# Second score matmul on 64 rows, two neighbouring tiles on the two halves of the array

## The chip, the cores and the metric

The kernel runs on one core of one Trainium2 chip. The metric is the device time of one execution in microseconds (us), here the median of 3 runs. Engines are named as in the profile: PE (TensorE matmul) and PEld (its weight loads), DVE (VectorE), ACT (ScalarE), POOL (GpSimd), SP (SyncE, which only issues transfers here).

## What is computed

An attention without softmax feeds two dense layers, one after the other, each of which widens 256 to 2048 columns and narrows back. Two batches of 3008 tokens go through it, in float32:

```python
scores = (1.0 / S) * np.matmul(z, z.transpose(0, 2, 1))   # z: (2, 3008, 64)
attn = np.maximum(scores, 0.0) ** 2
x = (u * np.matmul(attn, v)).reshape(B * S, D)            # u, v: (2, 3008, 256)
r = np.maximum(x @ moe_w_in, 0.0)                         # 256 -> 2048
x = (moe_s * (r * r) + moe_b) @ moe_w_out                 # 2048 -> 256
h = x @ moe2_w_in
out = (h * (1.0 / (1.0 + np.exp(-1.702 * h)))) @ moe2_w_out
```

Only the scores are touched by the change. The dot product behind a score has 64 terms, half of the array's 128 rows.

## The kernel before

**Two parts for each operand.** Matmul operands are of a rounded type (F32R). A value is therefore split into a high part (the value cast to F32R) and a low part (value minus high), and a product is summed from products of parts.

**Scores.** z of one batch is cut into 6 chunks of 512 tokens. `split_z` brings z of a chunk into `zt`, whose rows 0 to 63 and 64 to 127 both hold the transposed chunk. From it comes `zk`, the key operand: `high()` casts all 128 rows on ACT, and `low(cols)` (line 407) then subtracts in rows 64 to 127 on DVE, so that rows 0 to 63 hold the high part and rows 64 to 127 the low part of the same tokens. `queries` makes `zq`, the query operand, with two halves along the free axis: `zq[:, 0]` is the high part in both row halves, `zq[:, 1]` the low part in both. A score tile is 128 keys (tile t of 4 in chunk kc) by 512 queries (chunk c), built by two matmuls into one `ps` buffer (lines 566 to 568): with h = 0 the contraction over 128 rows gives (high + low of k) times high of q, with h = 1 it gives (high + low of k) times low of q.

**After the scores** (class `Fresh`, method `up`), each tile runs a chain: Relu with the scale, out of ps, on ACT (line 572); Square on ACT (575); the cast to the high part `hi` on ACT (582; on DVE, line 580, for the first four tiles); the low part `lo` on DVE (587, or 591 on half the rows for the last, short tile of a batch). For kc other than c, DVE also transposes the tile (616, method `turn`); four of them are parked in HBM and come back later as tile (kc, c) mirrored, for which class `Turned` only needs the two parts (666 on ACT, 670 on DVE). Method `down` then adds a tile's share of the output: `add_up` issues 6 matmuls (lines 507, 508, 512) into the accumulators accA or accB of the open session (one session is one query chunk). A tile's `down` is written 5 steps (`LAG`) behind its `up`.

**Order.** No engine's order is written by hand. `write_list` lists operations with costs, reads and writes (`put`, through `scalar`, `vector`, `matmuls`, `moves`), and `ordered` places them: a simulated clock for each engine, the PE line nearly in the order written (any of its next 16 operations that is ready may go), every other engine by what can start first, then by the latest due time. A negative `due` is added to an operation's latest time, a positive one replaces it. Buffers are counted too, among them 4 of kind `ps` and 56 `cell`. Decoding of the layers' weights (lines 716 to 803 on DVE, 719 and 794 on ACT) is `free` work, spread over 45 to 380 us for the first layer and 240 to 400 and 480 to 900 us for the second.

**Stages in the profile.** Attention of batch 0 fills the time up to about 230 us, that of batch 1 up to about 460 us. The first session of a batch has Fresh tiles only, and v of all chunks is split then (484 on ACT, 488 on DVE). Two dense layers follow.

Of the kernel before, what the change touches and what calls it, by code (L numbers as in the profile page):

```python
# [11 lines left out]
ALU = mybir.AluOpType  # L12
# [219 lines left out]
def attention_mlp_mlp_kernel(  # L232
# [13 lines left out]
    nc = tc.nc  # L246
# [3 lines left out]
    P = 128  # L250
# [75 lines left out]
    def vector(n, f, reads=(), writes=(), new=(), fast=False, **more):  # L326
        put("DVE", 0.065 + (0.00056 if fast else 0.00105) * n, 0.14, f, reads, writes, new, **more)
# [16 lines left out]
    def matmuls(count, n, f, reads=(), adds=(), writes=(), new=()):  # L344
        put("PE", count * (n / 2400 + 0.0133), 0.27, f, reads, writes, new, adds)
# [12 lines left out]
    def load_z(bb, t):  # L358
        n, z0, key = width(t), begin(bb, t), ("zr", bb, t)

        def tile_of():
            if key not in T:
                T[key] = cell(f"zr_{bb}_{t}").rearrange("p (t a) -> p t a", a=32)
            return T[key]

        fs = {"SP": [], "ACT": []}
        for i in range(4):
            q = slice(32 * i, 32 * i + 32)
            col = slice(32 * (i % 2), 32 * (i % 2) + 32)
            pieces = [(slice(0, n // 32), z0, n)]  # L370
            if n < CH:
                pieces.append((slice(n // 32, CH // 32), z0 + n - TAIL, TAIL))
            for cols, r0, r in pieces:
                on_act = (bb, t) == (0, 0) and i % 2

                def f(q=q, col=col, cols=cols, r0=r0, r=r, eng=nc.scalar if on_act else nc.sync):
                    eng.dma_start(
                        out=tile_of()[q, cols, :], in_=z[bb, r0 : r0 + r, col].rearrange("(t b) a -> b t a", b=32)
                    )

                fs["ACT" if on_act else "SP"].append(f)
        due = 0.0 if (bb, t) == (0, 0) else -16.0 if bb else None
        moves(64 * len(fs["SP"]), fs["SP"], (), [key], [(key, "cell")], run=128, due=due)
        if fs["ACT"]:
            moves(128, fs["ACT"], (), [(key, 1)], (), engine="ACT", run=128, due=due)

    def split_z(bb, t):
        zr, zt, zk = [(x, bb, t) for x in ("zr", "zt", "zk")]

        def turn():  # L390
            T[zt] = cell(f"zt_{bb}_{t}")
            if t < LASTC:
                nc.vector.transpose(
                    out=T[zt].rearrange("p (t g a) -> p t g a", t=4, g=4),
                    in_=T[zr].rearrange("p (g t) a -> p t g a", g=4),
                )
            else:
                nc.vector.transpose(out=T[zt], in_=T[zr].rearrange("p t a -> p (t a)"))

        def high():  # L400
            T[zk] = cell(f"zk_{bb}_{t}", F32R)
            if early and t:
                nc.vector.tensor_copy(out=T[zk], in_=T[zt])
            else:
                nc.scalar.copy(out=T[zk], in_=T[zt])

        def low(cols):
            nc.vector.tensor_tensor(out=T[zk][64:, cols], in0=T[zt][64:, cols], in1=T[zk][64:, cols], op=ALU.subtract)

        early = bb == 0 and t < EARLY  # L410

        vector(CH, turn, [zr] + ([(zr, 1)] if (bb, t) == (0, 0) else []), [zt], [(zt, "cell")])
        if (bb, t) == (0, 0):

            def go():
                nc.gpsimd.tensor_copy(out=going, in_=T[zt][:, :1])

            put("POOL", 0.1, 0.15, go, [zt], [("go",)])
        if early and t:
            vector(CH, high, [zt], [zk], [(zk, "cell")], fast=True)  # L420
        else:
            scalar(CH, high, [zt], [zk], [(zk, "cell")])
        if (bb, t) == (0, 0):
            vector(P, lambda: low(slice(0, P)), [zt, zk], [zk])
            vector(CH - P, lambda: low(slice(P, CH)), [zt, zk], [(zk, "rest")])
        else:
            vector(CH, lambda: low(slice(0, CH)), [zt, zk], [zk])

    def queries(bb, t):
        zt, zq = [(x, bb, t) for x in ("zt", "zq")]  # L430
# [12 lines left out]
    def load_v(bb, c):  # L443
        key, k0 = ("vr", bb, c), begin(bb, c)

        def tile_of():
            if key not in T:
                T[key] = big_tile(f"vr_{bb}_{c}").rearrange("p (t d) -> p t d", t=TPC)
            return T[key]

        pieces = []
        if c < LASTC:
            for g in range(4):
                pieces.append((slice(32 * g, 32 * g + 32), slice(0, TPC), k0 + g * P, P, "(t j) d -> j t d", dict(j=32)))
        else:
            pieces.append((slice(0, P), slice(0, 3), k0, 3 * P, "(t p) d -> p t d", dict(p=P)))
            for half in range(2):
                pieces.append((slice(64 * half, 64 * half + 64), slice(3, 4), k0 + 3 * P, TAIL, "(t p) d -> p t d", dict(p=TAIL)))
        first = (bb, c) == (0, 0)
        queue = "POOL" if bb == 0 and c else "SP"  # L460
        fs = {"SP": [], "ACT": [], "POOL": []}
        for x, (rows_, ts, r0, r, how, dims) in enumerate(pieces):
            issuer = "ACT" if first and x % 2 else queue

            def f(rows_=rows_, ts=ts, r0=r0, r=r, how=how, dims=dims, issuer=issuer):
                eng = dict(SP=nc.sync, ACT=nc.scalar, POOL=nc.gpsimd)[issuer]
                eng.dma_start(out=tile_of()[rows_, ts, :], in_=v[bb, r0 : r0 + r, :].rearrange(how, **dims))

            fs[issuer].append(f)
        due = 0.05 if first else None  # L470
        gate = [("go",)] if queue == "POOL" else []
        moves(128 * len(fs[queue]), fs[queue], gate, [key], [(key, "big")], engine=queue, run=1024, slow=1.5, due=due)
        if fs["ACT"]:
            moves(256, fs["ACT"], (), [(key, 1)], (), engine="ACT", run=1024, slow=1.5, due=due)
# [77 lines left out]
    class Fresh:  # L552
# [7 lines left out]
        def up(self):  # L560
            bb, n, kc, t, c = self.bb, self.n, self.kc, self.t, self.c
            zk, zq = ("zk", bb, kc), ("zq", bb, c)

            def scores():
                T[self.p] = ps.tile([P, CH], F32, tag=tag("ps"), name="ps_s")
                k = T[zk][:, t * P : (t + 1) * P]
                for h in range(2):
                    nc.tensor.matmul(T[self.p][:, :n], k, T[zq][:, h, :n], start=h == 0, stop=h == 1)  # L568

            def relu():  # L570
                T[self.a] = cell("a")
                nc.scalar.activation(out=T[self.a][:, :n], in_=T[self.p][:, :n], func=AF.Relu, scale=1.0 / S)  # L572

            def square():
                nc.scalar.activation(out=T[self.a][:, :n], in_=T[self.a][:, :n], func=AF.Square)  # L575

            def high():
                T[self.hi] = cell("hi", F32R)
                if first:
                    nc.vector.tensor_copy(out=T[self.hi][:, :n], in_=T[self.a][:, :n])  # L580
                else:
                    nc.scalar.copy(out=T[self.hi][:, :n], in_=T[self.a][:, :n])  # L582

            def low():
                T[self.lo] = cell("lo", F32R)
                a, hi, lo = [T[x][:, :n] for x in (self.a, self.hi, self.lo)]
                nc.vector.tensor_tensor(out=lo, in0=a, in1=hi, op=ALU.subtract)  # L587

            def low_half():
                hi = T[self.hi][64:, :n]  # L590
                nc.vector.tensor_tensor(out=hi, in0=T[self.a][64:, :n], in1=hi, op=ALU.subtract)

            early = (bb, kc, c) == (0, 0, 0)
            rest = [(zk, "rest")] if early and t else []
            matmuls(2, n, scores, [zk, zq] + rest, (), [self.p], [(self.p, "ps")])
            first = early and t < FIRST
            scalar(n, relu, [self.p], [self.a], [(self.a, "cell")])
            scalar(n, square, [self.a], [self.a])
            if first:
                vector(n, high, [self.a], [self.hi], [(self.hi, "cell")], fast=True)  # L600
            else:
                scalar(n, high, [self.a], [self.hi], [(self.hi, "cell")])
            if self.whole:
                vector(n, low, [self.a, self.hi], [self.lo], [(self.lo, "cell")])
            else:
                vector(n, low_half, [self.a, self.hi], [self.hi])
            if kc != c:
                self.turn()

        def turn(self):  # L610
            key, t = ("T", self.bb, self.kc, self.c), self.t
# [1089 lines left out]
```

## Time and profile before

| | us |
|---|---|
| median of 3 runs | 1388.39 (1387.8 to 1388.91) |
| the profiled execution | 1388.55 |
| its span, first to last instruction | 1386.5 |
| PE busy | 1377.9 |
| DVE busy | 1312.0 |
| ACT busy | 1187.4 |

The granted TensorE clock was 1.00 all through the span. Busy time of PE is time in which any matmul's record is open; records overlap, as the next matmul starts before the one ahead has left the array. The time of an execution is the span and some 2 us around it.

### The profile page before, as it was taken

The page shows a single profiled execution, that of the slowest core. Times are in us where ns is not written, and L with a number is a line of the kernel's source. Part 1 is how long each engine was busy: PE and PEld are TensorE (multiplying, and loading weights), DVE is VectorE, ACT ScalarE, POOL GpSimd, SP SyncE. Part 2 cuts the span into 40 slices and gives each one's busy share as a digit, 9 for nine tenths or more (in the row PEclk, how much of TensorE's full clock was granted, in tenths as well). Part 3 has the DMA queues.
Part 4 walks back from the last instruction along what each step waited for, and adds up shares of the span by engine and source line. Part 5 has one row for each costly group of instructions (what it writes and reads, how often), then busy time and mean ns, then how long its engine had stood idle before and what let it go on. Part 6 is the DMA issues. An engine that isn't in the chain of part 4 may idle for free.

```text
span 1386.5 us, 20220 instructions
## 1 busy us (share of the span) xinstructions
PE 1377.9 (99%) x6146; PEld 1149.4 (83%) x6146; DVE 1312.0 (95%) x2329; ACT 1187.4 (86%) x2304; POOL 197.4 (14%) x325
## 2 busy tenths in 40 slices
PE   9999999999999999999999999999999999999998
PEld 6788889888888888888888888988888888888897
DVE  8999999999999789999999999999999999999997
ACT  8999777999868698999989898988788796978785
POOL 4243221253321001001000100000010101010010
PEclk9999999999999999999999999999999999999999
DMA  9798998699998567677767575865767575655553
GB/s 198 241 285 272 304 279 218 184 306 279 294 312 295 177 214 254 209 234 260 271 218 249 189 267 193 288 219 202 237 212 262 171 259 166 235 183 200 178 186 107
DMA packets 187149, 322.62 MB, mean 233 GB/s; under 512 B 85408, under 2 KB 117728, under 8 KB 183200
## 3 DMA queue, kind: packets, MB, share of 16 engines
q1 hardware_dynamic: 160016, 241.68, 54.5%
q0 software_dynamic: 24288, 78.91, 17.4%
q10 hardware_dynamic: 2736, 0.74, 0.3%
q8 instruction: 49, 0.80, 0.2%
q14 instruction: 60, 0.49, 0.1%
HBM read 244.19 MB, written 77.07 MB: 232 GB/s over the span
## 4 chain that ended last, share of the span: by engine, by line
PE 99%; DVE 1%; ACT 0%; issue 0%; DVEq 0%
PE ps_b L1119 9%; PE ps_d L1119 9%; PE ps_c L1119 9%; PE accB L1312 7%; PE ps_b L1312 6%; PE ps_d L1312 6%; PE ps_s L568 5%; PE accA L508 5%; PE accA L507 5%; PE ps_a L1119 5%; PE accB L508 5%; PE accB L507 5%; PE accA L512 5%; PE accB L512 4%; PE ps_c L1312 4%; PE accA L1312 4%
## 5 line engine op out<-in xcount | busy, mean ns | idle before, releaser
L1242 DVE TENSOR_TENSOR lo<-g_c,hi 128x512 fp32r<-128x512 f32 (+1 forms) x540 | 344.9, 672 | 6.1 <-ACT hi L1238 5.3
L1238 ACT CAST hi<-g_c 128x512 fp32r<-128x512 f32 (+1 forms) x540 | 310.4, 616 | 10.6 <-DVE g_c L1227 9.0
L572 ACT ACTIVATE a<-ps_s 128x512 f32<-128x512 f32 (+1 forms) x168 | 102.7, 616 | 37.1 <-PE ps_s L568 36.8
L1119 PE MATMUL ps_b<-op_t,up 128*128 128x512 f32 (+1 forms) x432 | 120.6, 387 | 0.2 <-DVE g_c L1193 0.2
L1119 PE MATMUL ps_d<-op_t,up 128*128 128x512 f32 (+1 forms) x432 | 120.6, 387 | 0.0
L507 PE MATMUL accA<-hi,v 128*128 128x512 f32 x288 | 112.2, 390 | 0.9 <-DVE hi L580 0.9
L587 DVE TENSOR_TENSOR lo<-a,hi 128x512 fp32r<-128x512 f32 (+1 forms) x156 | 104.8, 672 | 8.5 <-ACT hi L582 7.9
L508 PE MATMUL accA<-hi,v 128*128 128x512 f32 x288 | 112.4, 390 | 0.1
L575 ACT ACTIVATE a<-a 128x512 f32<-128x512 f32 (+1 forms) x168 | 110.7, 660 | 0.6
L508 PE MATMUL accB<-hi,v 128*128 128x512 f32 (+1 forms) x288 | 109.8, 381 | 0.0
L507 PE MATMUL accB<-hi,v 128*128 128x512 f32 (+1 forms) x288 | 109.7, 381 | 0.0
L1205 ACT ACTIVATE g_c<-g_c 128x512 f32<-128x512 f32 (+1 forms) x144 | 89.3, 624 | 22.1 <-DVE g_c L1193 21.5
L1227 DVE TENSOR_TENSOR g_c<-g_c,g_c 128x512 f32<-128x512 f32 (+1 forms) x156 | 105.1, 674 | 1.3
L582 ACT CAST hi<-a 128x512 fp32r<-128x512 f32 (+1 forms) x164 | 105.3, 643 | 0.5
L568 PE MATMUL ps_s<-zq,zk 128*128 128x512 f32 (+1 forms) x336 | 102.3, 389 | 0.1
L1312 PE MATMUL accB<-hi,d 128*128 128x512 f32 (+1 forms) x312 | 95.0, 386 | 0.0
L1119 PEld LDWEIGHTS ps_b<-op_t,up 128*128 128x128 f32 x432 | 80.1, 188 | 17.3 <-DVE g_c L1193 1.4
L1119 PEld LDWEIGHTS ps_d<-op_t,up 128*128 128x128 f32 x432 | 79.8, 188 | 17.4 <-ACT s_u L1168 2.1
L1208 ACT ACTIVATE g_c<-g_c 128x512 f32<-128x512 f32 (+1 forms) x144 | 88.7, 630 | 0.5
L635 POOL DMA_DIRECT2D H<-T x120 | 66.1, 557 | 137.9 <-DVE T L616 115.5
L512 PE MATMUL accA<-lo,v 128*128 128x512 f32 x276 | 85.1, 390 | 0.0
L616 DVE STREAM_TRANSPOSE T<-a 128x512 f32<-128x512 f32 x120 | 84.0, 702 | 0.2
(180 smaller groups left out, 3479.2 us busy)
## 6 DMA issues: line engine op xcount, KB each, us to landing
up<-uf SPq DMA_DIRECT2D x96, 896.0 KB
H<-T POOLq DMA_DIRECT2D x120, 256.0 KB, 6.3
R<-H SPq DMA_DIRECT2D x30, 1024.0 KB
d<-dw SPq DMA_DIRECT2D x114, 256.0 KB
d_s<-df1s SPq DMA_DIRECT2D x54, 256.0 KB
d_s<-df0s SPq DMA_DIRECT2D x72, 128.0 KB
f<-rows SPq DMA_DIRECT2D x18, 512.0 KB
d_s<-df0s SPq DMA_DIRECT2D x36, 256.0 KB
```

Source lines behind the costliest of these rows:

```text
L507: nc.tensor.matmul(T[k][:, :n], w[:, 0, cols], T[hi][:, :n], **start_flags(k, fresh))
L508: nc.tensor.matmul(T[k][:, :n], w[:, 1, cols], T[hi][:, :n], **start_flags(k, ()))
L512: nc.tensor.matmul(T[k][:, :n], w[:, 0, cols], T[lo][:, :n], **start_flags(k, ()))
L568: nc.tensor.matmul(T[self.p][:, :n], k, T[zq][:, h, :n], start=h == 0, stop=h == 1)
L575: nc.scalar.activation(out=T[self.a][:, :n], in_=T[self.a][:, :n], func=AF.Square)
L582: nc.scalar.copy(out=T[self.hi][:, :n], in_=T[self.a][:, :n])
L587: nc.vector.tensor_tensor(out=lo, in0=a, in1=hi, op=ALU.subtract)
L1119: nc.tensor.matmul(to[:, :n], a[h], y[:, g, :n], start=first and j == 0, stop=False, skip_group_check=True)
L1227: nc.vector.tensor_tensor(out=self.get(to), in0=self.get(x), in1=self.get(y), op=ALU.subtract)
L1238: nc.scalar.copy(out=T[keys[0]][:, :n], in_=self.get(c))
L1242: nc.vector.tensor_tensor(out=T[keys[1]][:, :n], in0=self.get(c), in1=T[keys[0]][:, :n], op=ALU.subtract)
L1312: nc.tensor.matmul(to[:, :n], w[:, h, cols], g[:, :n], start=first and j == 0, stop=False, skip_group_check=True)
```

## The change

A tile's second score matmul (h = 1) uses 64 rows alone: the high part of k times the low part of q. The product of the two low parts, which rows 64 to 127 had added, is dropped. So that the second matmuls of two neighbouring tiles can name different halves of the array, odd tiles of a chunk have their parts in `zk` the other way round: `low(odd)` subtracts in rows 0 to 63 for odd tiles and in rows 64 to 127 for even ones, as two instructions of 256 columns (three for the first chunk). The even tile's `scores` issues only its full matmul. The odd tile's issues its own full one, then the even tile's second on rows 0 to 63, then its own second on rows 64 to 127. The chain behind both tiles (`later`) is listed after the odd tile's scores, the even tile's first. For the planner the even tile's operation counts one matmul, the odd one's two. Due times of the first z and v transfers become -100 and -50 instead of 0 and 0.05.

```diff
-        due = 0.0 if (bb, t) == (0, 0) else -16.0 if bb else None
+        due = -100.0 if (bb, t) == (0, 0) else -16.0 if bb else None
...
-        def low(cols):
-            nc.vector.tensor_tensor(out=T[zk][64:, cols], in0=T[zt][64:, cols], in1=T[zk][64:, cols], op=ALU.subtract)
+        def low(odd, xs=slice(0, 2)):
+            rows_ = slice(0, 64) if odd else slice(64, 128)
+            to, src = [T[x][rows_].rearrange("p (x y k) -> p y x k", y=2, k=P)[:, odd, xs] for x in (zk, zt)]
+            nc.vector.tensor_tensor(out=to, in0=src, in1=to, op=ALU.subtract)
...
-            vector(P, lambda: low(slice(0, P)), [zt, zk], [zk])
-            vector(CH - P, lambda: low(slice(P, CH)), [zt, zk], [(zk, "rest")])
+            vector(P, lambda: low(0, slice(0, 1)), [zt, zk], [zk])
+            vector(HALF, lambda: low(1), [zt, zk], [(zk, "rest")])
+            vector(P, lambda: low(0, slice(1, 2)), [zt, zk], [(zk, "rest")])
         else:
-            vector(CH, lambda: low(slice(0, CH)), [zt, zk], [zk])
+            for odd in range(2):
+                vector(HALF, lambda odd=odd: low(odd), [zt, zk], [zk])
...
-        due = 0.05 if first else None
+        due = -50.0 if first else None
...
+            def product(x, rows_, h):
+                k = T[zk][rows_, x.t * P : (x.t + 1) * P]
+                nc.tensor.matmul(T[x.p][:, :n], k, T[zq][rows_, h, :n], start=h == 0, stop=h == 1)
+
             def scores():
                 T[self.p] = ps.tile([P, CH], F32, tag=tag("ps"), name="ps_s")
-                k = T[zk][:, t * P : (t + 1) * P]
-                for h in range(2):
-                    nc.tensor.matmul(T[self.p][:, :n], k, T[zq][:, h, :n], start=h == 0, stop=h == 1)
+                product(self, slice(0, P), 0)
+                if t % 2:
+                    product(other, slice(0, 64), 1)
+                    product(self, slice(64, P), 1)
...
+            def later():
+                scalar(n, relu, [self.p], [self.a], [(self.a, "cell")])
+                scalar(n, square, [self.a], [self.a])
...
             early = (bb, kc, c) == (0, 0, 0)
+            first = early and t < FIRST
             rest = [(zk, "rest")] if early and t else []
-            matmuls(2, n, scores, [zk, zq] + rest, (), [self.p], [(self.p, "ps")])
-            first = early and t < FIRST
-            scalar(n, relu, [self.p], [self.a], [(self.a, "cell")])
-            scalar(n, square, [self.a], [self.a])
...
+            other = self.session.steps[self.session.steps.index(self) - 1] if t % 2 else None
+            matmuls(2 if t % 2 else 1, n, scores, [zk, zq] + rest, [other.p] if t % 2 else (), [self.p], [(self.p, "ps")])
+            self.later = later
+            if t % 2:
+                other.later()
+                later()
```

## Rows read from the trace of the kernel before

**Rows 1.** The page: busy us (share) of each engine; the chain that ended last.
```profile
PE 1377.9 (99%) x6146; PEld 1149.4 (83%) x6146; DVE 1312.0 (95%) x2329; ACT 1187.4 (86%) x2304; POOL 197.4 (14%) x325
...
PE 99%; DVE 1%; ACT 0%; issue 0%; DVEq 0%
```

**Rows 2.** Windows: length, then busy us (xinstructions) of PE, PEld, DVE, ACT, POOL.
```profile
50.00:100.00 50.00, 50.00 (x222) 41.41 (x221) 49.84 (x96) 48.39 (x94) 17.62 (x31) 1.00 0.85 259
100.00:250.00 150.00, 150.00 (x680) 127.16 (x679) 142.00 (x273) 118.89 (x234) 37.17 (x61) 1.00 0.90 268
250.00:300.00 50.00, 50.00 (x222) 41.44 (x221) 49.88 (x104) 49.64 (x104) 18.18 (x32) 1.00 0.77 236
300.00:450.00 150.00, 150.00 (x672) 125.71 (x671) 143.43 (x271) 124.46 (x239) 44.91 (x72) 1.00 0.94 293
450.00:500.00 50.00, 50.00 (x232) 42.89 (x231) 38.32 (x72) 34.16 (x65) 1.96 (x3) 1.00 0.53 186
500.00:930.00 430.00, 429.83 (x1924) 359.68 (x1923) 422.59 (x738) 400.95 (x777) 29.48 (x44) 1.00 0.70 238
```

**Rows 3.** Timeline at 54 us: start, length, engine, line, operation.
```profile
54.09 0.62 PE L568 MATMUL ps_s<-zq,zk 128*128 128x512 f32 x2
...
54.54 0.39 PE L507 MATMUL accA<-hi,v 128*128 128x512 f32 x1
54.55 0.19 PEld L508 LDWEIGHTS accA<-hi,v 128*128 128x128 f32 x1
```

**Rows 4.** Instructions of the ps_s tiles: Relu, one for each score tile (ns, starts, forms).
```profile
L572 ACT ACTIVATE a<-ps_s x168: 536/600/737, 7.8 to 444.7; 128x512 f32<-128x512 f32 x160, 128x448 f32<-128x448 f32 x8
```

**Rows 5.** Timeline at 10 us: a matmul that waited, and the next one.
```profile
9.99 0.50 PE L507 MATMUL accA<-hi,v 128*128 128x512 f32 x1 [0.88 <-DVE hi L580]
...
10.33 0.40 PE L508 MATMUL accA<-hi,v 128*128 128x512 f32 x1
```

**Rows 6.** Timeline at 490 us: four matmuls of 64 columns, and the next load.
```profile
490.17 0.53 PE L900 MATMUL ps_c<-ones,wt 128*128 128x64 f32 x4
...
490.50 0.30 PEld L1312 LDWEIGHTS accB<-hi,d 128*128 128x128 f32 x2
```

**Rows 7.** Timeline of ACT, 19 to 50 us: the first and the last of 16 Relus.
```profile
21.64 0.60 ACT L572 ACTIVATE a<-ps_s 128x512 f32<-128x512 f32 x1
...
49.56 0.66 ACT L572 ACTIVATE a<-ps_s 128x512 f32<-128x512 f32 x1
```

**Rows 8.** Windows of line 568 alone: length, busy us (xmatmuls), loads, clock, DMA.
```profile
0.00:50.00 50.00, 15.68 (x52) 9.53 (x52) 1.00 0.90 218
...
250.00:300.00 50.00, 16.62 (x54) 10.13 (x54) 1.00 0.77 236
```

**Rows 9.** DVE groups from 250 to 300 us: busy us, mean ns, idle before.
```profile
L803 DVE TENSOR_TENSOR forms<-wf,forms 128x256 fp32r<-128x256 f32 (+2 forms) x6 | 2.7, 447 | 0.0
L781 DVE TENSOR_TENSOR ws<-wf 128x128 f32<-128x128 f32 x8 | 2.1, 278 | 0.0
```

**Rows 10.** Timeline of the first 10 us: from the first transfers to the first lo.
```profile
0.74 0.91 SPq L377 DMA_DIRECT2D zr<-in_z_dram  x2
...
1.70 0.95 SPq L467 DMA_DIRECT2D vr<-in_v_dram  x2
...
6.51 0.76 DVE L408 TENSOR_TENSOR zk<-zt,zk 64x128 fp32r<-64x128 f32 x2
...
6.91 2.20 PE L568 MATMUL ps_s<-zq,zk 128*128 128x512 f32 x8
...
7.76 1.09 ACT L572 ACTIVATE a<-ps_s 128x512 f32<-128x512 f32 x2 [0.34 <-PE ps_s L568]
...
9.97 0.69 DVE L587 TENSOR_TENSOR lo<-a,hi 128x512 fp32r<-128x512 f32 x1
```

**Rows 11.** Lines 408 and 488 on DVE: count, min/median/max ns, first and last start.
```profile
L408 DVE TENSOR_TENSOR zk<-zt,zk x13: 289/690/692, 6.5 to 261.9; 64x512 fp32r<-64x512 f32 x11, 64x128 fp32r<-64x128 f32 x1, 64x384 fp32r<-64x384 f32 x1
...
L488 DVE TENSOR_TENSOR v<-vr,v x48: 379/417/426, 7.3 to 279.2; 128x256 fp32r<-128x256 f32 x48
```

More of the change, by code (lines that the diff above doesn't have):

```diff
@@ L591, in low_half @@
                 nc.vector.tensor_tensor(out=hi, in0=T[self.a][64:, :n], in1=hi, op=ALU.subtract)
+            def later():
+                scalar(n, relu, [self.p], [self.a], [(self.a, "cell")])
+                scalar(n, square, [self.a], [self.a])
+                if first:
+                    vector(n, high, [self.a], [self.hi], [(self.hi, "cell")], fast=True)
+                else:
+                    scalar(n, high, [self.a], [self.hi], [(self.hi, "cell")])
+                if self.whole:
+                    vector(n, low, [self.a, self.hi], [self.lo], [(self.lo, "cell")])
+                else:
+                    vector(n, low_half, [self.a, self.hi], [self.hi])
+                if kc != c:
+                    self.turn()
             early = (bb, kc, c) == (0, 0, 0)
+            first = early and t < FIRST
             rest = [(zk, "rest")] if early and t else []
-            matmuls(2, n, scores, [zk, zq] + rest, (), [self.p], [(self.p, "ps")])
-            first = early and t < FIRST
-            scalar(n, relu, [self.p], [self.a], [(self.a, "cell")])
-            scalar(n, square, [self.a], [self.a])
[L599 to L608, printed above, removed]
+            other = self.session.steps[self.session.steps.index(self) - 1] if t % 2 else None
[4 more added lines that the diff above has]
+                later()
         def turn(self):
```

## The prediction, made before the changed kernel was run

> **What bounds the kernel now.** I read the page's busy shares and its chain of work first [rows 1]: PE is busy for 1377.9 of 1386.5 us, and the chain that ended last is PE for 99%. The windows by stage [rows 2] then show PE without a hole from 50 to 500 us, so each slot of PE that goes in the attention stage is worth its full length, as long as ACT and DVE keep up. That is the second thing to see in these rows: between 50 and 100 us and between 250 and 300 us ACT and DVE are nearly full too (49.64 and 49.88 of 50 us in the latter), while from 100 to 250 us ACT has 31 of 150 us idle.
>
> The timeline gives the price of one slot [rows 3]: the two score matmuls of a tile start at 54.09 and the next matmul at 54.54, so one takes 0.227 us from start to start, though a matmul's own record lasts 0.39: 0.16 us are pipeline that the next one overlaps. A Fresh tile (score and its share of the output) is 8 slots, 1.81 us.
>
> **The change part by part.** Times are set against the profiled execution, 1388.55 us (span 1386.5 and 2.05 around it); the median of the runs, 1388.39, is the same within 0.02%.
>
> *Slots removed.* There are 168 score tiles, so 336 score matmuls and 84 pairs [rows 4]. A pair now has 4 full matmuls in 4 slots. Afterwards it has 2 full ones and 2 of 64 rows that name different halves of the array. If these two run at the same time, a pair takes 3 slots: 84 x 0.227 = 19.0 us of PE less (8 tiles, four of the pairs, are 448 wide, which takes 0.1 off: 18.9).
>
> *What two half-row matmuls cost.* No matmul of the trace uses fewer than 128 rows, so I bound it. Lower end: one slot for both, 0.227. Upper end without any penalty: two slots, 0.454, nothing saved. Between them lies the weight load. In the flow before, the next load starts at the moment the current matmul starts (54.55 beside 54.54 [rows 3]), so one load is hidden per slot. What a load costs when nothing hides it: the matmul at 9.99 had waited for DVE, its load with it, and the next matmul came at 10.33, that is 0.34 instead of 0.227, so 0.11 us [rows 5]; the four matmuls of only 64 columns say the same, from the first one's start at 490.17 to the load of what follows at 490.50 three more of them pass, 0.11 us each [rows 6]. If the load of the second half can't start before the first half's matmul has, the pair of halves takes 0.11 + 0.227 = 0.34, and the saving is 0.117 per pair. If both loads go under the full matmul ahead of them, they take 0.22 of its 0.227 us and it just fits. I take the lower end, one slot, since the two loads fit by these rows and write different rows; the 0.34 is a rival.
>
> *Changing between 128 and 64 rows.* This happens twice per pair and no row shows it. Below nothing it can't be, since a changeover removes no work. The nearest row for its upper end is a matmul's record beside its spacing [rows 3]: were the pipeline run empty at each change, 0.39 - 0.227 = 0.16 us each, 0.32 per pair, which is more than the 0.227 saved. With the weight load uncovered as well it is 0.11 more each, 0.54 per pair. I take zero, because [rows 3] show consecutive matmuls with different weights and different outputs overlapping their tails with no gap, and I keep the upper end for the range.
>
> The Trainium skill speaks on both sides here. Its page "TensorEngine Tiling (Array Packing)", Key Properties, says that a change of tiling mode, not just of tile, drains TensorE; by that rule the sum would be the slower rival below. "TensorE: Matmul & The Clock Gate", Part 3, The mechanism, says that matmuls on different row groups start about 4 ns apart and that loads overlap running matmuls where the row group differs; by that the pair is one slot. No row here shows either.
>
> *Where ACT stands in the way.* In the first session the tile needs, on ACT, Relu, Square, a cast, a cast of v and a quarter of a cast of zk. ACT's timeline shows no idle gap between the Relu that starts at 21.64 and the one at 49.56, with 14 others between, so 27.92 / 15 = 1.86 us per tile [rows 7]. PE's 1.81 would become 1.70, but ACT's 1.86 stays. The 52 score matmuls up to 50 us, 13 pairs [rows 8], therefore cash nothing: 13 x 0.227 = 2.9 us lost, 16.0 left. From 250 to 300 us (54 matmuls, 13.5 pairs [rows 8]) ACT and DVE are as full, but there part of it is decoding of weights with late due times (lines 719 and 794 on ACT, 726 to 803 on DVE, of which two groups alone make 4.8 us in that window [rows 9]), which the planner can put off. DVE has 8.0 + 0.1 + 6.6 + 11.7 = 26.4 us idle between 100 and 500 us [rows 2] to take it; after 500 it has hardly any (7.4 of 430). So the gain is between all of it and none of the 13.5 pairs here and of about as many from 50 to 100 us: 0 to 6.1 us lost. I take the middle, 3 us, since neither end is nearer.
>
> *The start.* Tile 0's Relu now waits for tile 1's scores, and these wait for two more subtractions on DVE. Before, the first subtraction is at 6.51, the first score at 6.91, the Relu at 7.76 [rows 10]. Two more DVE instructions of 0.3 us and one slot less ahead of it put the Relu some 0.6 us later; PE idles 0.88 us there already for the first tile [rows 5], so all of it shows: 0.6 lost. The earlier due times of z and v keep the order that these first transfers already have (z at 0.74, v at 1.70 [rows 10]); nothing.
>
> *Moved and small things.* In each of 11 chunks one 64x512 subtraction (0.69 us) becomes two of half the columns; by the 256-column instruction (0.42) these take 0.84 at most, 0.15 more [rows 11]: 1.7 us of DVE in all, in the 26.4 idle; what of it falls where DVE is full lies inside the 3 us above. The even tile's Relu, Square, casts and transposition are issued after the odd tile's scores, so its ps buffer is held one step longer, 1.8 us, and its lead before its output matmuls shrinks from five steps (9 us) to four (7.2). From Relu to the end of lo takes 2.9 us on the first tile (7.76 to 9.97 + 0.69 [rows 10]), so it is covered unless ACT's queue is longer than 4 us. Behind that waiting Relu on ACT stand the other tiles' casts; the planner orders them by readiness, so I cost the wait at nothing, and in the first session it is part of ACT's bound.
>
> Sum: -18.9 + 2.9 + 3.0 + 0.6 = -12.4 us, 1388.5 - 12.4 = 1376 us. Its own bounds: without losses at ACT and DVE except the start 1370.2, with all of them 1379.2.
>
> **The rivals.** (1) *The weight load between the halves.* 0.117 us per pair, 71 pairs outside the first session: 8.3, less 1.0 for crowding and 0.6 for the start: 1382. For it: [rows 3, 6], where never more than one load stands ahead of a running matmul. Against: those loads all use the whole array, so they had no free rows to go to.
> (2) *The change does not do what it says:* the two halves run one after the other. Then PE does the same 4 slots, and only the start is lost: 1389. A partial emptying that eats just the 0.227 gives the same.
> (3) *Slower: the array empties at each change of rows.* 2 x 0.16 - 0.227 = +0.10 us per pair, from the point where a change costs more than 0.113 us; 84 pairs give 8.1, with the start 0.6: 1397. With loads uncovered too, 0.31 per pair, it would be 1415. For it: nothing in the trace mixes row counts, so nothing excludes it. Against: no gap between any two matmuls that change weights, moving operand and output at once [rows 3].
>
> **How the numbers follow.** The forecast (both halves in one slot, no costly change) 0.42; rival 1 0.22; rival 2 with partial emptying 0.12; rival 3 0.24. The predicted time is the forecast's, 1376. Range: 1370 (no crowding) to 1396 (the near end of rival 3); left out is most of rival 3's far side and a little below, under 2 in 10. A difference under 0.2% (2.8 us) can't be told from none here. Faster by more than that: the forecast and nearly all of rival 1, less crowding worse than assumed: 0.62. Same: rival 2 and the edges of 1 and 3: 0.13. Slower: 0.25. The range of the likeliest alone is 1370 to 1379.
>
> **What would show it.** In the changed trace, the second half-row matmul starting within some 10 ns of the first shows one slot; 0.11 us apart shows rival 1; 0.227 shows rival 2; a gap of 0.1 us or more ahead of the first half-row matmul, or ahead of the first full one behind, shows rival 3. ACT without a gap and holes on PE up to 50 us show the first session's bound; in the windows from 250 to 300 us holes on PE behind DVE or ACT show crowding. The prediction is wrong if PE's holes at ACT run on past the first session, or if PE's slots in the attention stage do not shrink by a quarter of the scores.

## The result, and the profile after

| | before | after |
|---|---|---|
| median, us | 1388.65 | 1409.1 |
| profiled execution, span, us | 1388.55, 1386.5 | 1409.13, 1407.3 |
| PE, DVE, ACT busy, us | 1377.9, 1312.0, 1187.4 | 1397.4, 1312.7, 1185.7 |

The medians are those of 4 executions each. The changed kernel is slower: ratio 1.0149, 95% interval 1.0131 to 1.0166, 20.5 us. The forecast was 1376.

The page of the changed kernel first, the lines that answer to [rows 1]. Of the chain only 92% is PE now; nearly all that left PE lies between 600 and 950 us, in the dense layers, so the chain tells nothing of the scores.

```profile
PE 1397.4 (99%) x6146; PEld 1126.8 (80%) x6146; DVE 1312.7 (93%) x2341; ACT 1185.7 (84%) x2304; POOL 197.4 (14%) x325
...
PE 92%; DVE 5%; ACT 1%; DMA 1%; issue 1%; SPq 0%; DVEq 0%; ACTq 0%
```

PE runs as many matmuls as before and is busy 19.5 us longer, so the loss lies in PE's own stream and not in long waits. The windows that answer to [rows 2] (length; PE, PEld, DVE, ACT, POOL busy us) say where:

```profile
50.00:100.00 50.00, 50.00 (x212) 36.48 (x211) 45.23 (x86) 44.77 (x89) 17.18 (x29) 1.00 0.84 262
100.00:250.00 150.00, 150.00 (x659) 117.76 (x658) 134.66 (x259) 111.02 (x219) 32.10 (x53) 1.00 0.83 248
250.00:300.00 50.00, 50.00 (x211) 35.45 (x209) 47.80 (x95) 48.61 (x102) 14.46 (x25) 1.00 0.69 212
300.00:450.00 150.00, 150.00 (x642) 113.97 (x643) 140.04 (x267) 120.54 (x235) 48.81 (x79) 1.00 0.90 282
500.00:930.00 430.00, 428.99 (x1911) 356.74 (x1910) 421.51 (x744) 401.34 (x776) 32.59 (x49) 1.00 0.71 239
```

In the attention stage PE gets through 212 matmuls in the first 50 us shown where it was 222, and DVE has 4.8 us idle where it had 0.2. PE's own busy time does not tell why, as it is full as before. The loads do: those that belong to the scores have an idle time before them that no engine ends (us in total, times, longest):

```profile
PEld ps_s L570 <- issue: 29.7, 86, 0.4
```

And one pair in the timeline of the load engine, which shows the starts of consecutive loads (two of 64 rows merged into one row) and the idle time before them:

```profile
53.04 0.19 PEld L570 LDWEIGHTS ps_s<-zq,zk 128*128 128x128 f32 x1
53.58 0.19 PEld L570 LDWEIGHTS ps_s<-zq,zk 64*128 64x128 f32 x2 [0.35 <-issue]
54.01 0.19 PEld L511 LDWEIGHTS accA<-hi,v 128*128 128x128 f32 x1 [0.24 <-issue]
54.12 0.19 PEld L512 LDWEIGHTS accA<-hi,v 128*128 128x128 f32 x1
```

Read it with the matmul rows of the same stretch:

```profile
53.26 0.82 PE L570 MATMUL ps_s<-zq,zk 128*128 128x512 f32 x3
54.01 0.50 PE L511 MATMUL accA<-hi,v 128*128 128x512 f32 x1
```

The odd tile's full matmul starts at 53.26. In the flow of [rows 3] the next load would start then as well; here it starts at 53.58, 0.32 us later, which is the matmul's slot of 0.227 and 0.09 more. Both 64-row loads start together and take one load's time. No matmul's slot covers them: the load at 54.01 comes 0.43 after them, which is a load of 0.11, a slot of 0.227 and again 0.09. (By its record, 0.39 long, the full matmul is still open for 0.07 us when the half-row loads start; such ends are modelled, so whether the array is empty by then is not shown.) The full matmul behind waits for its own uncovered load, 0.11, as its follower's load at 54.12 shows (its record lasts 0.50, like the waiting one of [rows 5]). So from 53.26 to 54.12 it is 0.86 us, where three slots take 0.68. A changeover costs 0.09 + 0.11 = 0.20 us; two of them 0.40; a slot of 0.227 is saved. Over all pairs that are 512 wide the median of this distance is 0.856, so the loss is 0.174 us per pair, 84 x 0.174 = 14.6 us.

The rest shows when the first and last rows of the dense layers' first line are compared, before and after (count; ns; first and last start):

```profile
L1119 PE MATMUL ps_b<-op_t,up x432: 362/389/481, 462.1 to 1357.5; 128*128 128x512 f32 x120, 128*128 128x448 f32 x24
```

```profile
L1135 PE MATMUL ps_b<-op_t,up x432: 358/389/504, 478.5 to 1378.3; 128*128 128x512 f32 x120, 128*128 128x448 f32 x24
```

The dense layers start 16.4 us later and, though no instruction of theirs changed, last 899.8 instead of 895.4 us, 4.4 more. Most of these 4.4 are lost while weights are still decoded. Set back by the 16.4 us, the window that was 500 to 930 in [rows 2] has 1912 matmuls where it had 1924, 12 slots or some 2.7 us:

```profile
516.40:946.40 430.00, 428.69 (x1912) 356.83 (x1911) 424.38 (x750) 401.82 (x778) 31.34 (x48) 1.00 0.72 242
```

### The profile page after: what moved, and what is told of

It reads as the page before. It is cut to its first block, busy times and chain, and to the rows that moved or that the text cites. A ratio compares the mean times of both kernels' runs of the same rounds, so it can differ in the third digit from the quotient of the medians.

```text
span 1407.3 us, 20225 instructions
## 1 busy us (share of the span) xinstructions
PE 1397.4 (99%) x6146; PEld 1126.8 (80%) x6146; DVE 1312.7 (93%) x2341; ACT 1185.7 (84%) x2304; POOL 197.4 (14%) x325
## 4 chain that ended last, share of the span: by engine, by line
PE 92%; DVE 5%; ACT 1%; DMA 1%; issue 1%; SPq 0%; DVEq 0%; ACTq 0%
PE ps_d L1135 9%; PE ps_c L1135 8%; PE ps_b L1135 8%; PE accB L1328 7%; PE ps_b L1328 6%; PE ps_s L570 5%; PE accA L511 5%; PE accB L511 5%; PE accA L512 5%; PE accB L512 5%; PE accA L516 4%; PE accB L516 4%; PE ps_a L1135 4%; PE ps_d L1328 4%; PE accA L1328 3%; PE ps_c L1328 3%
## 5 line engine op out<-in xcount | busy, mean ns | idle before, releaser
L581 ACT ACTIVATE a<-ps_s 128x512 f32<-128x512 f32 (+1 forms) x168 | 92.9, 603 | 57.7 <-PE ps_s L570 57.3
L511 PE MATMUL accA<-hi,v 128*128 128x512 f32 x288 | 117.5, 408 | 1.1 <-DVE hi L589 1.1
L511 PE MATMUL accB<-hi,v 128*128 128x512 f32 (+1 forms) x288 | 113.4, 394 | 0.0
L512 PE MATMUL accA<-hi,v 128*128 128x512 f32 x288 | 112.6, 391 | 0.0
L512 PE MATMUL accB<-hi,v 128*128 128x512 f32 (+1 forms) x288 | 110.2, 383 | 0.0
L584 ACT ACTIVATE a<-a 128x512 f32<-128x512 f32 (+1 forms) x168 | 101.4, 642 | 0.0
L570 PE MATMUL ps_s<-zq,zk 128*128 128x512 f32 (+2 forms) x336 | 99.9, 445 | 0.1
L591 ACT CAST hi<-a 128x512 fp32r<-128x512 f32 (+1 forms) x164 | 98.1, 632 | 0.1
```

The source lines that it names most:

```text
L511: nc.tensor.matmul(T[k][:, :n], w[:, 0, cols], T[hi][:, :n], **start_flags(k, fresh))
L512: nc.tensor.matmul(T[k][:, :n], w[:, 1, cols], T[hi][:, :n], **start_flags(k, ()))
L570: nc.tensor.matmul(T[x.p][:, :n], k, T[zq][rows_, h, :n], start=h == 0, stop=h == 1)
```

## The experiments

Every kernel was timed beside the kernel before on the same chip; that one's median was 1388.35 to 1388.48 in the three groups.

**Is it the change of rows?** First the changed kernel with both second matmuls on all rows (e2_full_rows):

```diff
-                    product(other, slice(0, 64), 1)
-                    product(self, slice(64, P), 1)
+                    product(other, slice(0, P), 1)
+                    product(self, slice(0, P), 1)
...
-            matmuls(2 if t % 2 else 1, n, scores, ...)
+            matmuls(3 if t % 2 else 1, n, scores, ...)
```

> The changed kernel with both second matmuls on all 128 rows (so the product of the two low parts is added again) and the planner counting 3 for the odd tile: pairing, layout of the parts in zk and the late chain stay, but no matmul changes the row count. Theory (the change of rows is what costs): the time of the kernel before plus the start, 1389 to 1390 us. Rival (the pairing and the chain that starts later cost a good part of it): over 1395 us.

Measured: 1393.6 us, ratio 1.0038 (1.0023 to 1.0053). Between the two expectations: 15.5 us of the loss go with the 64 rows, near the 14.6 of the timeline, but 5.2 us stay without them. In the profiled execution (1396.15, the slowest of the four) the loss lies in the attention stage: the dense layers start 7.1 us later than before and last 895.0 us, as before.

```profile
L1135 PE MATMUL ps_b<-op_t,up x432: 362/389/499, 469.2 to 1364.2; 128*128 128x512 f32 x120, 128*128 128x448 f32 x24
```

These are the longer of its waits of PE up to 500 us; the list of the kernel before has only two, both at the start (1.2 us, which e2 has too, and 0.9 for the first hi):

```profile
PE accB L516 <- DVE lo L596: 1.8, 1, 1.8
PE accA L512 <- DVE v L492: 1.7, 4, 0.6
...
PE accA L511 <- DVE hi L589: 1.1, 1, 1.1
PE accA L511 <- ACT a L584: 1.1, 1, 1.1
```

The changed kernel has none of the others: its own list has just the two at the start. So the 5.2 us here and the 4.4 us that it loses in its dense layers are different losses, and that the difference to e2 comes out so near the timeline's price is in part luck. The timeline and the next experiment carry the argument, not this difference.

Next, the opposite: the kernel before, with its order and plan untouched, and only the second matmul cut to 64 rows (e5_alone):

```diff
                 for h in range(2):
-                    nc.tensor.matmul(T[self.p][:, :n], k, T[zq][:, h, :n], start=h == 0, stop=h == 1)
+                    r = slice(0, 64 if h else P)
+                    nc.tensor.matmul(T[self.p][:, :n], k[r], T[zq][r, h, :n], start=h == 0, stop=h == 1)
```

> The kernel before with one edit: each tile's second matmul uses rows 0 to 63 alone, where every tile has its high part (the product of the two low parts is left out, as in the changed kernel). No pairing, order and plan as before, but the row count changes around each of the 168 second matmuls instead of around 84 pairs. Theory (a change into 64 rows costs 0.09 us of waiting and an uncovered load of 0.11, the change back the same): a tile takes 0.40 us more, 168 x 0.40 = 67 us, 1455 us, a few less where PE waits for ACT anyway. Rival (the cost belongs to the pairing and to two outputs written side by side, not to the row count): 1389 us.

Measured: 1453.0 us, ratio 1.0462, 64.5 us more for 168 times in and out. The load engine's timeline repeats the pattern of the pair with one 64-row load in it:

```profile
100.31 0.19 PEld L569 LDWEIGHTS ps_s<-zq,zk 128*128 128x128 f32 x1
100.85 0.18 PEld L569 LDWEIGHTS ps_s<-zq,zk 64*128 64x128 f32 x1 [0.35 <-issue]
101.28 0.19 PEld L507 LDWEIGHTS accB<-hi,v 128*128 128x128 f32 x1 [0.24 <-issue]
101.39 0.19 PEld L508 LDWEIGHTS accB<-hi,v 128*128 128x128 f32 x1
```

The same 0.35 and 0.24 us of idle time, with no neighbour, no second output and no other order. The row count alone makes the price, 0.40 us for in and out: 168 x 0.40 = 67, of which 64.5 show. The dense layers last 894.9 us here: with the plan of the kernel before they lose nothing.

**Do the halves run side by side?** Two edits of the changed kernel: both second matmuls on rows 0 to 63 (e3_same_half), and the odd tile's left out (e4_one_half; its full matmul then closes the sum). The diff is that of e3; in e4 the line falls away.

```diff
-                    product(self, slice(64, P), 1)
+                    product(self, slice(0, 64), 1)
```

> The changed kernel with both second matmuls on rows 0 to 63 (the odd tile then adds low times low instead of high times low). Theory (in the changed kernel the two halves run at the same time): the second now has to wait for the first, 84 x 0.227 = 19 us more if its weight load is hidden, 84 x 0.334 = 28 us more if it is not: 1428 to 1437 us. Rival (the halves gain nothing from being different halves): 1409 us.

> The changed kernel without the odd tile's second matmul, which leaves that part of its score out. Theory (the halves run side by side and the price is per change of rows): the gaps stay as they are and the time too, 1408 to 1410 us. Rival (each half-row matmul costs its own time): 84 x 0.227 = 19 us less, 1390 us.

Measured: 1425.9 us for the same half, 16.8 more than the changed kernel, a little under what was expected; 1406.5 without the second, 2.7 less, where 19 would have been its own slot. So yes: on different halves the second one is nearly free, on the same half it costs a slot.

Nearly, as the matmul records show a small drag. Behind a pair of the changed kernel, the first full matmul and the one after it start 0.338 us apart and the next four starts follow at 0.235, 0.235, 0.232 and 0.232 (medians), 0.031 us more in all than in e4 and e5, where a single half-row matmul is followed by 0.333 and then 0.227 at once. With the 3 ns by which the second half starts later that is 84 x 0.034 = 2.9 us, the 2.7 of e4. In e3, with two on the same half, most of it is there too, so it goes with the second half-row matmul and not with the change of rows; why was not tested.

In e3 the two loads are no longer side by side, yet the second is covered by the first's matmul:

```profile
100.74 0.29 PEld L570 LDWEIGHTS ps_s<-zq,zk 64*128 64x128 f32 x2 [0.35 <-issue]
101.40 0.19 PEld L511 LDWEIGHTS accB<-hi,v 128*128 128x128 f32 x1 [0.36 <-issue]
```

From the first 64-row load to the next full one it is 0.66, against 0.43 in the pair: one slot of 0.227 more and no load.

**Is the price per change or per matmul?** Four tiles in place of two (e7_quads); `four` are the tiles of a chunk, known when the last of them comes, and all four chains are listed behind it:

```diff
-    LAG = 5
+    LAG = 7
...
-                if t % 2:
-                    product(other, slice(0, 64), 1)
-                    product(self, slice(64, P), 1)
+                if t == TPC - 1:
+                    for x in four:
+                        product(x, slice(64, P) if x.t % 2 else slice(0, 64), 1)
...
-            matmuls(2 if t % 2 else 1, n, scores, ...)
+            matmuls(5.3 if four else 1, n, scores, ...)
...
```

> The changed kernel with four neighbouring tiles instead of two: their four full matmuls at their places, then the four half-row ones behind the last of them, alternating between the halves; outputs are added 7 steps behind instead of 5, and the planner is told the price. Row counts change 84 times in place of 168. If the price is per change alone, four tiles take 4 + 2 slots + 0.41 = 1.77 us, 0.05 less than in the kernel before, 42 x 0.05 = 2 us less on PE. If a half-row load can't be covered by a matmul on the same half (the third matmul then starts 0.335 after the first instead of 0.227), four tiles take 1.88 us and PE loses 2.7 us. Holds of four ps buffers at a time may add holes on PE at ACT: 1386 to 1400 us.

Measured: 1401.4 us, ratio 1.0091 (1.0071 to 1.0111), just above the expected range. The load engine, one group of four:

```profile
107.39 0.30 PEld L570 LDWEIGHTS ps_s<-zq,zk 64*128 64x128 f32 x4 [0.35 <-issue]
108.05 0.19 PEld L511 LDWEIGHTS accA<-hi,v 128*128 128x128 f32 x1 [0.36 <-issue]
108.16 0.19 PEld L512 LDWEIGHTS accA<-hi,v 128*128 128x128 f32 x1
```

Four half-row matmuls take 0.66 from load to load, one slot more than two of them, and the second couple's loads are covered by the first couple's matmuls. The price is per change: a group of four tiles takes 0.68 for the first three full matmuls, 0.32 from the fourth to the first half-row load and 0.77 from there to the load at 108.16, 1.77 us, 0.05 less than in the kernel before, 2 us in all, of which the drag behind a group, 0.03 us as behind a pair, takes 1.3. What is left is more than lost again: PE stands still 4.3 us for zk in the first session, and the dense layers start 6.6 us later than before and last 902.0 us, 6.6 more:

```profile
PE ps_s L570 <- DVE zk L410: 4.3, 2, 3.7
```

```profile
L1135 PE MATMUL ps_b<-op_t,up x432: 362/389/500, 468.7 to 1370.7; 128*128 128x512 f32 x120, 128*128 128x448 f32 x24
```

That holding four ps buffers at a time does this, as expected, is not shown: for Relu, which frees them, PE waits 0.3 us.

**Where do the other 5 us come from?** First guess: the planner believed PE faster than it was, put decoding of weights off, and the dense layers paid. One of the lines of DVE's decoding (729 before, 745 after) has 8 instructions between 500 and 930 us before and 10 after:

```profile
L729 DVE SCALAR_TENSOR_TENSOR pw<-wr,pw 128x512 uint32<-128x512 uint32 x8 | 5.5, 686 | 0.0
```

```profile
L745 DVE SCALAR_TENSOR_TENSOR pw<-wr,pw 128x512 uint32<-128x512 uint32 x10 | 6.8, 682 | 0.0
```

Two kernels test the belief from both sides: the changed kernel with the true price (e1_told), and the kernel before with the false one (e6_misplanned; the changed due times are in it too, but put alone into the kernel before they give the very same program, so they can't be a cause here or below).

```diff
-            matmuls(2 if t % 2 else 1, n, scores, ...)     (changed kernel)
+            matmuls(3.77 if t % 2 else 1, n, scores, ...)  (e1)
-            matmuls(2, n, scores, ...)                     (kernel before)
+            matmuls(1.5, n, scores, ...)                   (e6)
```

> The changed kernel with one number edited: the planner counts the odd tile's operation as 3.77 matmuls (its measured 0.855 us) instead of 2. Theory: changes of row count cost 84 x 0.174 = 14.6 us on PE, and the other 6 us come from a plan that believed PE to be faster than it is, put decoding of weights off into the dense layers and made PE wait there for DVE. Then the dense layers take no longer than before and the time is 1388.6 + 14.6 + 0.5 at the start = 1404 us. Rival: the dense layers lose because the pairs of tiles come in another order, whatever the planner believes: 1408 to 1410 us.

> The kernel before with the planner told that a tile's two score matmuls cost 1.5 (the changed kernel's belief), and the changed due times of the first transfers; every instruction is the same, only their order may differ. Theory (a wrong belief about PE puts decoding off into the dense layers, which cost the changed kernel 4.3 us more than before from the end of attention on): 1391 to 1393 us, the loss lying in the dense layers. Rival (the order does not suffer from the belief): 1389 us.

Measured: e1 1408.6 us (1.0147, 1.0130 to 1.0163), no better than the changed kernel; e6 1392.0 us (1.0024, 1.0014 to 1.0033). The kernel with the false belief takes 3.5 us more, as expected, and in the dense layers, as expected: they last 899.1 us from first to last row, and like the changed kernel's they have 1912 matmuls between 500 and 930 us.

```profile
L1119 PE MATMUL ps_b<-op_t,up x432: 362/389/500, 462.4 to 1361.5; 128*128 128x512 f32 x120, 128*128 128x448 f32 x24
```

But the truth does not give it back: e1's dense layers still last 897.8 us, and its median is where it was. So the belief isn't the whole cause, if it is one at all. Another kernel takes the changed split of z alone (e8_layout: the changed `low`, its instructions and due times, with the score matmuls and chains of the kernel before), and two take the smallest change of plan that was at hand (e10_cost205, e11_cost195: the kernel before with 2.05 or 1.95 instead of 2 in the planner's cost, and the changed due times).

> The kernel before with the changed split of z alone (two subtractions per chunk, three in the first, odd tiles' parts the other way round) and the changed due times; both score matmuls of a tile use all rows and follow each other as before. The full-row version of the changed kernel took 5 us more than before. Theory (that comes from tiles waiting for their neighbour): 1389 us here. Rival (it comes from the extra DVE instructions, since DVE is full in the first sessions): 1393 us.

> The kernel before with the planner told 2.05 instead of 2 for a tile's two score matmuls, and the changed due times (which alone leave the order as it was). Every instruction is the same; the order shifts by a belief that is off by 0.011 us per tile. Theory A (a replanned order costs only as far as the belief is wrong): 1388 to 1389 us. Theory B (the order before is a lucky one, and any other plan of the same work costs 2 to 4 us, which is then what the changed kernel loses beside its row changes): 1390 to 1393 us.

> The same with 1.95 instead of 2.05. Theory A: 1388 to 1389 us. Theory B: 1390 to 1393 us.

Measured:

| | us | ratio, 95% interval |
|---|---|---|
| e8_layout | 1392.2 | 1.0026 (1.0017 to 1.0036) |
| e10_cost205 | 1392.8 | 1.0035 (1.0025 to 1.0045) |
| e11_cost195 | 1390.9 | 1.0016 (1.0007 to 1.0025) |

The same instructions, in orders planned with a belief that differs by 0.011 us per tile, cost 4.4 us (e10) and 2.6 us (e11) more. Single executions of e10 go from 1390.6 to 1395.9, those of the kernel before on the same chip from 1387.7 to 1390.1. So the order of the kernel before is a favourable one: the three other orders of the same instructions that were run (e6, e10, e11) lost 2.6 to 4.4 us to it, about as much as the 4.4 that the changed kernel loses in its dense layers. That another order is what costs there too is the likeliest reading, but it was not isolated. The 3.7 us of e8 lie in the same span, so its extra DVE instructions need not cost anything, but they are not cleared either. The profiled executions of e8 and e10 are the fastest of theirs, so their traces don't show where the medians lose. What part of e2's 5.2 us is the waiting of even tiles for odd ones, and which place in an order makes it good, was not separated.

## Why the prediction was wrong

The failed step is *Changing between 128 and 64 rows*, where I took zero: "because [rows 3] show consecutive matmuls with different weights and different outputs overlapping their tails with no gap". Those rows have only matmuls of the same row count, so they bear on a change of weights and not on a change of rows; the nearest row was not near. A change costs 0.20 us (0.09 of waiting beyond the running matmul's slot, 0.11 for a load that was not covered), twice per pair; e5 shows it without anything else changed. The bounds that I had written down, 0 to 0.54 us per pair, did hold the 0.40. The point from which the change loses was written down too, 0.113 us per changeover, and lies below the 0.20. What I did with them was wrong twice: the likeliest case was put at the one end that the change needed, and the range ended at 1396, as the near end of rival 3, which by its own sum is 1397 and has the load covered, for which there was no row either; here it is not covered. With 2 x (0.09 + 0.11) - 0.227 = 0.173 us per pair and the 0.6 for the start, rival 3 gives 1388.5 + 14.5 + 0.6 = 1404. It had the direction right; the 5 us from there to 1409 have other causes.

The Trainium skill's page "TensorEngine Tiling (Array Packing)", Key Properties, said that a change of tiling mode drains TensorE. The trace bears out that such a change is not free, with 0.09 us of waiting and a load of 0.11 that stays uncovered, each way; as the load starts 0.07 us before the modelled end of the matmul ahead, it does not show a full drain. The Trainium skill's page "TensorE: Matmul & The Clock Gate", Part 3, The mechanism, gives about 4 ns between the starts of matmuls on different row groups; the records of the pairs have 3 to 4 ns.

Point by point:

- *One slot for the two halves* was right: starts 3 to 4 ns apart, loads side by side, e3 and e4. Rival 1 and the first form of rival 2 fall with it; the second form, an emptying that eats just the 0.227, falls with the 0.40. The argument for it, two loads of 0.11 hidden one behind the other under the full matmul ahead, was wrong: none is hidden there, and the two take the time of one.
- *The saving of 18.9 us* is thus real, less 2.6 us of drag, and is paid back by 84 x 0.40 = 34 us of changes.
- *The first session's bound at ACT*: it did not show in the changed kernel, whose PE did not become faster. In e2 PE waits four times, 1.7 us in all, for the low parts of v on DVE (line 492), two of these in each batch's first session, and once, 1.1 us, for ACT (line 584): no bound at ACT alone, and none that was looked for by an experiment.
- *Crowding of DVE and ACT*, 3 us, was not tested by the change either: with PE slower, DVE had more idle time, 4.8 us from 50 to 100 us.
- *The start*, 0.6 us: the first output matmul is at 10.34 instead of 9.99 [rows 5], 0.35.
- *No term at all* stood for the plan. That every engine's order follows from the costs was described, and I costed only what the changed instructions do. Another order of the same instructions was worth 2.6 to 4.4 us here.

The sum as measured: 14.6 us for the rows (the changes less the slots saved), some 2.6 for the drag behind the pairs and 0.35 at the start, 17.5 together where the dense layers start 16.4 us later; and 4.4 us in the dense layers, for which another order of the same work is likely and not shown.

## What to carry to other kernels

Half-row matmuls on the two halves of the array do run side by side, but getting into that shape and out of it costs 0.2 us each way here, about a matmul of 512 columns for both together and most of another: group enough of them that what is saved exceeds 0.4 us, which a pair, saving 0.227, can't, and which four tiles, saving 0.454, only just do, with most of it lost to the drag. A row of the trace bounds a new cost only if it differs from the new case in nothing that the cost may hang on; where it does differ, keep the far end in the range and ask which end the change needs to be true. And where a planner makes the order, a change of one cost is a change of the whole order: measure the same work replanned before a difference of a few us is ascribed to an instruction.

## What the runs showed of the hardware

- A change of row count waits 0.09 us beyond the running matmul's slot. The matmul's record, 0.39, would have let one expect 0.16.
- The load behind such a change is uncovered (0.11 us), but between matmuls of 64 rows loads are covered again, with the running matmuls on the same half (e3) or on both (e7).
- Two 64-row loads for different halves take the time of one; their starts are 3 to 4 ns apart.
- A group of two half-row matmuls is followed by full ones that start 0.235 to 0.232 us apart for four starts, before 0.227 is back; a single one is not (e4, e5). What makes it is open.
